# Three edits to a fused attention, feed-forward and soft-expert kernel: when query chains begin, which TensorE work goes first, and where the short key sums stand

## The chip, the cores and the metric

The kernel runs on one core of a Trainium2 chip. The time is the device time of one execution in microseconds (us), the median of three runs. A profile is one more execution, taken by the hardware profiler; its times are its own and are compared with its own total.

## The reference

Three stages follow each other, on 4 x 1088 = 4352 tokens of 128 numbers.

- **Attention by feature maps.** For each of 4 batches and 4 heads, a query or key x of 32 numbers becomes 64 features, phi(x) = outer(S1 x, S2 x), with S1 and S2 of 8 x 32. The keys of a batch are summed up once, kv = sum over the sequence of phi(k) v and z = sum of phi(k); a query's answer is phi(q) kv / (phi(q) z + 1e-6). The sequence of 1088 is 8 x 128 + 64, so each key sum has eight full pieces of 128 rows and one short piece of 64.
- **Gated feed-forward.** x is scaled by its root mean square, then silu(x Wg) * (x Wv) is formed with 1536 hidden numbers and multiplied by Wo back to 128.
- **Soft experts.** logits = x phi with 32 slots; a softmax over all tokens gives each slot's input, 8 experts of two layers process 4 slots each, and a softmax over slots mixes the results for each token. The maximum over all tokens means that this stage ends after the last token of the second.

## The kernel before

The tokens are cut into nine tiles: T = 0 to 7 hold 512 tokens each (two tiles to a batch), and T = 8 holds the 256 that are left over from all batches. A tile's feed-forward runs in 12 slots, one for each 128 hidden columns (`NF` = 12; six double ones for T = 8). In a slot TensorE makes `g` and `v`, three passes of 512 columns each (`mm3`, L692 to L694: high by high, low by high, high by low parts of float32 as two float32r numbers). ScalarE makes `silu` of g (L733) and the rounded `hh` (L743), VectorE the product `hf` (L734) and the rest `hl` (L748), and two slots later TensorE adds three more passes into the output `o`. In tile 0 the output uses whole float32 products instead (L758). So a slot holds nine full matmuls of 128 x 128 weights and 512 columns.

Beside these slots run generators called chains, which are advanced one step at a time; each step says on which phase the next one goes, `PE` or `POST` (the other engines), and how many slots later.

- `k_chain(b)` prepares a batch's keys: VectorE transposes (L366), TensorE projects (L385, L389), VectorE forms the products `work` and `pkr` (L318), TensorE sums them with v (L424, method `sum`; `work` are the full pieces, `pkr` the short ones), ScalarE spreads the sums (L435), TensorE transposes them (L449) and ScalarE places them in `kvz` (L458).
- `q_chain(T)` prepares a tile: VectorE transposes the queries (L542), TensorE projects (L547), VectorE forms the products (L318) and transposes them, TensorE multiplies by `kvz` (`attend`, L579, or L587 for T = 8), VectorE divides (L595 to L598), ScalarE squares (L621), GpSimd takes the root (L628, L629), VectorE scales (L634), TensorE transposes (L640), and ScalarE and VectorE write `xh` and `xl` (L647, L653), which every `g` and `v` of that tile reads.
- `r_chain(T)` makes the logits of a finished tile (L775, L792).

`start_tile(T)`, called in a tile's first slot, issues the loads of the next batch on even T, spawns its key chain, and spawns the query chain of tile T + 1. Tile 0's own chains are written out in the list `FRONT`.

The small TensorE work of a chain step is called a burst here. The engine executes its instructions in the order of its queue, and that order is set when the kernel is built: a scheduler picks among instructions whose predecessors are done by its own estimate, by priority, which is by default the order in which the code was written. `tc.issue_after(i)` keeps an instruction behind i on the engine; `tc.high_priority()` puts it ahead of others that are ready. The function `burst` (L936) runs a chain's PE step behind the burst before it. Only the `attend` of L579 has the higher priority before the change.

Of the kernel before, what the change touches and what calls it, by code (L numbers as in the profile page):

```python
# [21 lines left out]
NF = DFF // P  # L22
# [15 lines left out]
WORDS = "1 2 3 3 3 3 3 4 4 4 3 3 4 4 5 5 5 4 5 5 4 6 6 6 6 6 7 7 7 6 6 7 7 8 8 8 7 8 8 7"  # L38
CONV = 6
LOCK = 3  # L40

WHOLE = NF

PIECE = 256
PE, POST = "pe", "post"
# [4 lines left out]
def body(ctx, tc, q, k, v, s1, s2, wg, wv, wo, rg, phi, w1, w2, out):  # L50
# [19 lines left out]
    def row(tag, bufs=1, dt=F32):  # L70
        return sb.tile([P, 512], dt, tag=tag, name=tag, bufs=bufs)
# [123 lines left out]
    mark = {}  # L195
# [147 lines left out]
    def bank():  # L343
        if not free:
            return aux()
        free.append(free.pop(0))
        tag = free[-1]
        return ps.tile([P, 512], F32, tag=tag, name=tag, bufs=3 if tag == "aux" else 2)

    class Keys:  # L350
# [25 lines left out]
        def project(self, banks=1):  # L376
            for h in range(H):
                if h == 0 or h == 2 and banks == 2:
                    a = bank()
                self.a["k", h // 2] = a  # L380
                cs = slice(P * h, P * h + P)
                for c in range(2) if banks == 2 else (1, 0):
                    with tc.issue_after(self.last) if self.last else nullcontext():
                        o = a[64 * c : 64 * c + 64, cs]
                        self.last = pe.matmul(o, bdk.rearrange("p h r -> p (h r)"), self.kT[c][:, cs], start=True, stop=True).ins  # L385

        def project_r(self):
# [24 lines left out]

        def sum(self, hp, ts, banks=1):

            for t in ts:
                if t == 0 and (hp == 0 or banks == 2):
                    self.a["kv", hp] = self.a["kv"] = bank()
                if banks == 1:
                    self.a["kv", hp] = self.a["kv"]

                for h2 in range(2):
                    h = 2 * hp + h2
                    v0 = D1 * (8 * h + 4 * (t % 2) + t // 2) if t < 8 else D1 * h
                    pe.matmul(  # L424
                        self.a["kv", hp][64 * h2 : 64 * h2 + self.cols, 64 * hp : 64 * hp + 64],
                        (va_all if t < 8 else vr_all)[:, v0 : v0 + self.cols],
                        self.pk[hp][:, h2, t, :] if t < 8 else self.pk[2][:64, h, 0, :],
                        start=(t == 0),
                        stop=(t == 8),
                    )  # L430

        def spread(self):
# [45 lines left out]
    def k_chain(b):  # L478
        k = Keys(b)
        with tc.issue_after(mark["word"]), tc.issue_after(mark["pow"]):  # L480
            k.zero()
            if b == 1:
                pool.memset(kvT[32:64], 0.0)
            for hp in range(2):
                k.copy_v(hp, pool.tensor_copy)
        for c in (0, 1):
            yield POST, 1
            with tc.issue_after(mark["gate"]):
                k.transpose(c)
                if c == 0:  # L490
                    k.transpose(2)
        yield PE, 0
        k.project_r()
        k.project()
        kv_done.discard("free")
        yield POST, 1
        k.turn(slice(0, 2), row("x2"))
        k.halves_r()
        mark["k"] = k.outer(2)
        kv_done.add("free")  # L500
        k.outer(0)
        yield POST, 1
        k.outer(1)
        yield PE, 0
        for hp in range(2):
            k.sum(hp, range(9))
        yield PE, 1
        yield POST, 0
        k.spread()
        yield PE, 0  # L510
        k.back()
        yield POST, 1
        k.place()
        kv_done.add(b)
# [391 lines left out]
    def spawn(c, phase, at=0):  # L906
        chains.append([c, phase, now + at])
# [25 lines left out]
    def burst(*step):  # L933
        traced = nc.cur_bb.bb.instructions
        start = len(traced)
        with tc.issue_after(mark["burst"]) if "burst" in mark else nullcontext():  # L936
            step[0](*step[1:])
        for i in traced[start:]:
            if i.engine == mybir.EngineType.PE:
                mark["burst"] = i  # L940
# [62 lines left out]
    def after_front():  # L1003
        s = ExitStack()
        if now < base + LOCK:
            for i in front_end.values():
# [6 lines left out]
    def start_tile(T):  # L1013
        if T == 6:
            for u in range(2):
                for hf in range(2):
                    load(
                        out=qr[64 * hf : 64 * hf + 64, :, u, :], in_=q[2 * u + hf, :, 1024:, :].rearrange("h p d -> p h d")
                    )
        if T == 2:  # L1020
            with tc.issue_after(mark["word"]), tc.issue_after(mark["pow"]):
                make_own()
                pool.tensor_copy(phi4[:, 1:4], phi4[:, 0:1].to_broadcast([P, 3, NS]))
        if T % 2 == 0 and T // 2 + 1 < B:
            b = T // 2 + 1
            load_k(b)
            load_q(b)
            load_kr(b)
            load_v(b)
            spawn(k_chain(b), PE, 8 if b == 1 else 0)  # L1030
        if T < 8:
            spawn(q_chain(T + 1), POST, 2 if T == 0 else 0)
        else:
            w = work()[:, 0 : 2 * DM].rearrange("p (c n) -> p c n", n=DM)
            h, l = (t[:, NF - 2 :, :].bitcast(F32) for t in (woh, wol))
            pool.tensor_tensor(out=w, in0=h, in1=l, op=ALU.add)
            wo_end.extend((w[:, 0], w[:, 1]))
        if 6 <= T <= 7:
            for e in range(4 * (T - 6), 4 * (T - 6) + 4):
                if e < 5:  # L1040
                    t = ring()
                    load(out=t, in_=w1[e])
                    w1_sb[e] = [t[:, 0:512], t[:, 512:]]
                else:
                    w1_sb[e] = [row(("cvs", "cvc", "cvt")[e - 5], 2) for _ in range(2)]
                    for c in range(2):
                        load(out=w1_sb[e][c], in_=w1[e, :, 512 * c : 512 * c + 512])
            for j in range(2 * (T - 6), 2 * (T - 6) + 2):
                for c in range(2):
                    t = ring() if j < 3 else big("qt", 2)  # L1050
                    w2_sb[j, c] = t.rearrange("p (e c n) -> p e c n", e=2, c=4)
                    for e in range(2):
                        src = w2[4 * e + j, 512 * c : 512 * c + 512]
                        load(out=w2_sb[j, c][:, e], in_=src.rearrange("(c p) n -> p c n", p=P))
# [4 lines left out]
    for i in range(n_slots + LAG):  # L1059
        now = base + i  # L1060
        if i < n_slots:
            T, f = slots[i]
            if "silu" in mark:
                mark["pace"] = mark["silu"]
            ff_in(T, f)
            if f == 0:
                start_tile(T)
        if i == NF - 1:
            conv.append(split_o())
        if i == 0:  # L1070
            ordered[:] = [mybir.EngineType.DVE]
            for e in list(latest):
                if e not in ordered:
                    latest.pop(e)
        if i == 2:
            ordered.clear()
            latest.clear()
        if 1 <= i <= n_slots:
            in_order(ff_low, *slots[i - 1])
        for _ in range(CONV if i else 0):  # L1080
            with after_front():
                in_order(conv_step, 1)
        if i < n_slots:
            in_order(ff_gate, T, f)
            mark.setdefault("pace", mark["silu"])
        for _ in range(0 if i else CONV):
            with after_front():
                in_order(conv_step, 1)
        for c in list(chains):
            with after_front():  # L1090
                in_order(advance, POST, c)
        if i < n_slots:
            in_order(ff_high, T, f)
        if i >= LAG:
            To, fo = slots[i - LAG]
            in_order(ff_out, To, fo)
            if fo == NF - 1 and To < 8:
                if To < 7:
                    spawn(r_chain(To), POST, 1)
                else:  # L1100
                    with tc.high_priority():
                        for _ in r_chain(To):
                            pass
                        a_max()
        for c in list(chains):
            with after_front():
                burst(in_order, advance, PE, c)
# [25 lines left out]
    b, c = aux(), ps.tile([P, 512], F32, tag="v", name="c", bufs=2)  # L1133
# [122 lines left out]
    for o, part, eng in zip(sod, (soh, sol), (act.copy, dve.tensor_copy)):  # L1256
# [7 lines left out]
        for t in range(2):  # L1264
            ts = slice(64 * t, 64 * t + 64)
# [69 lines left out]
```

## Time and profile before

| | us |
|---|---|
| median of 3 runs | 310.29 (310.04 to 311.12) |
| the profiled execution | 309.8 |
| its span, first to last instruction | 307.8 |
| TensorE busy | 297.0 |
| VectorE busy | 235.0 |
| ScalarE busy | 179.1 |
| GpSimd busy | 65.7 |

The profiled execution is 2.0 us longer than the span that its trace covers. A TensorE matmul's row runs from its start to the modelled end of its results, so that rows overlap; how long one holds the engine is read from its start to the next one's start. A float32 matmul stands in the trace as two passes, so x2 of the order is x4 of the trace; the float32r ones of L692 to L694 and the transposes are one.

### The profile page before, as it was taken

What the parts mean: (1) busy time and instruction counts of PE and PEld (TensorE: products, weight loads), DVE (VectorE), ACT (ScalarE), POOL (GpSimd) and SP (SyncE); (2) the same over time, 40 slices, a digit from 0 to 9 for tenths busy, and PEclk for the clock granted to TensorE, in tenths of its full rate; (3) what the DMA queues carried; (4) which work ended last, traced back from release to release, by engine and by line L of the source; (5) the groups of instructions that cost most, each with busy time, mean ns of one, the idle gap of its engine ahead of it and who ended that gap; (6) DMA issues with size and microseconds to landing.
All of it is one profiled execution on the core that took longest, in us unless ns stands there. A gap on an engine that the chain in (4) does not pass through costs nothing.

```text
span 307.8 us, 6343 instructions
## 1 busy us (share of the span) xinstructions
PE 297.0 (96%) x2372; PEld 231.7 (75%) x2372; DVE 235.0 (76%) x461; ACT 179.1 (58%) x400; POOL 65.7 (21%) x111
## 2 busy tenths in 40 slices
PE   7999989999999999999999989999999999999993
PEld 4777655787887778788878867888787878897482
DVE  3989956877888967978699779787985767665862
ACT  2568774476565376755653667556654665466562
POOL 2569899000602010110020200102000000003210
PEclk9999999999999999999999999999999999999998
DMA  5997000010025100010351001001981692000016
GB/s 143 348 337 214 9 1 0 2 24 13 0 78 151 26 2 0 15 21 0 81 152 19 0 3 23 13 0 27 350 205 19 173 320 53 2 0 3 2 51 240
DMA packets 40766, 24.02 MB, mean 78 GB/s; under 512 B 18080, under 2 KB 36768, under 8 KB 40736
## 3 DMA queue, kind: packets, MB, share of 16 engines
q1 hardware_dynamic: 40560, 23.56, 26.7%
q8 instruction: 18, 0.29, 0.4%
q10 hardware_dynamic: 176, 0.07, 0.1%
q14 instruction: 12, 0.10, 0.1%
HBM read 19.81 MB, written 2.23 MB: 72 GB/s over the span
## 4 chain that ended last, share of the span: by engine, by line
PE 78%; DVE 7%; ACT 5%; POOL 4%; issue 2%; DMA 1%; SPq 1%; DVEq 0%; ACTq 0%; POOLq 0%
PE g L692 7%; PE v L692 7%; PE v L693 7%; PE g L693 7%; PE g L694 7%; PE v L694 7%; PE o L694 6%; PE o L692 6%; PE o L693 6%; PE o L758 2%; PE aux L579 2%; POOL wgl L277 2%; PE aux L424 2%; DVE work L318 2%; PE fo L1286 2%
## 5 line engine op out<-in xcount | busy, mean ns | idle before, releaser
L743 ACT CAST hh<-hf 128x512 fp32r<-128x512 f32 x89 | 54.9, 617 | 46.6 <-DVE hf L734 46.1
L733 ACT ACTIVATE silu<-g 128x512 f32<-128x512 f32 (+1 forms) x103 | 60.1, 592 | 36.2 <-PE g L694 35.6
L734 DVE TENSOR_TENSOR hf<-v,silu 128x512 f32<-128x512 f32 (+1 forms) x91 | 61.2, 676 | 16.6 <-PE v L694 6.4
L748 DVE TENSOR_TENSOR hl<-hf,hh 128x512 fp32r<-128x512 f32 x89 | 60.7, 686 | 14.5 <-ACT hh L743 12.7
L692 PE MATMUL g<-xh,wgh 128*128 128x512 f32 (+1 forms) x107 | 43.7, 408 | 1.8 <-ACT xh L647 0.9
L692 PE MATMUL v<-xh,wgh 128*128 128x512 f32 (+1 forms) x107 | 42.6, 398 | 0.4 <-DVE hh L734 0.4
L693 PE MATMUL g<-xh,wgl 128*128 128x512 f32 (+1 forms) x107 | 41.0, 383 | 0.0
L694 PE MATMUL v<-xl,wgh 128*128 128x512 f32 (+1 forms) x107 | 40.7, 380 | 0.0
L693 PE MATMUL v<-xh,wgl 128*128 128x512 f32 (+1 forms) x107 | 40.5, 379 | 0.0
L694 PE MATMUL g<-xl,wgh 128*128 128x512 f32 (+1 forms) x107 | 40.5, 379 | 0.0
L694 PE MATMUL o<-hl,woh 128*128 128x512 f32 (+1 forms) x94 | 36.8, 392 | 0.0
L692 PE MATMUL o<-hh,woh 128*128 128x512 f32 (+1 forms) x94 | 36.6, 389 | 0.0
L693 PE MATMUL o<-hh,wol 128*128 128x512 f32 (+1 forms) x94 | 35.7, 380 | 0.0
L628 POOL TENSOR_SCALAR rs<-ss 128x4 f32<-128x4 f32 (+1 forms) x8 | 2.8, 354 | 123.3 <-ACT sq L621 123.2
L692 PEld LDWEIGHTS g<-xh,wgh 128*128 128x128 f32 x107 | 20.1, 188 | 8.5 <-ACT silu L733 2.8
L692 PEld LDWEIGHTS v<-xh,wgh 128*128 128x128 f32 x107 | 20.1, 188 | 5.8 <-DVE hh L734 1.2
L693 PEld LDWEIGHTS g<-xh,wgl 128*128 128x128 f32 x107 | 20.1, 188 | 4.7 <-POOL wgl L277 0.6
L694 PEld LDWEIGHTS g<-xl,wgh 128*128 128x128 f32 x107 | 20.1, 188 | 4.1 <-issue 0.2
L694 PEld LDWEIGHTS v<-xl,wgh 128*128 128x128 f32 x107 | 20.1, 188 | 4.0
L693 PEld LDWEIGHTS v<-xh,wgl 128*128 128x128 f32 x107 | 20.2, 188 | 3.4 <-issue 0.2
L694 PEld LDWEIGHTS o<-hl,woh 128*128 128x128 f32 x94 | 17.8, 189 | 3.9 <-DVE hl L748 0.4
L692 PEld LDWEIGHTS o<-hh,woh 128*128 128x128 f32 x94 | 17.7, 189 | 3.3 <-issue 0.2
(278 smaller groups left out, 492.8 us busy)
## 6 DMA issues: line engine op xcount, KB each, us to landing
ring<-in_moe_w_dram SPq DMA_DIRECT2D x12, 256.0 KB, 6.6
ring<-in_moe_w_dram SPq DMA_DIRECT2D x5, 512.0 KB, 4.6
ring<-in_k_dram SPq DMA_DIRECT2D x16, 128.0 KB, 3.0
ring<-in_v_dram SPq DMA_DIRECT2D x4, 512.0 KB, 5.4
ring<-in_moe_w_gate_dram SPq DMA_DIRECT2D x6, 256.0 KB, 5.1
ring<-in_moe_w_val_dram SPq DMA_DIRECT2D x6, 256.0 KB, 7.6
ring<-in_moe_w_out_dram SPq DMA_DIRECT2D x3, 512.0 KB, 7.9
qt<-in_q_dram SPq DMA_DIRECT2D x3, 512.0 KB
```

Source lines behind the costliest of these rows:

```text
L277: i = pool.tensor_tensor(out=dl[:, ts], in0=src[:, ts], in1=dh[:, ts].bitcast(F32), op=ALU.subtract)
L318: return on.tensor_tensor(out=dst.rearrange("p g (r s) -> p g r s", s=R), in0=x1.unsqueeze(3).to_broadcast([pp, n, r, R]), in1=x2.unsqueez ...
L424: pe.matmul(self.a["kv", hp][64 * h2 : 64 * h2 + self.cols, 64 * hp : 64 * hp + 64], (va_all if t < 8 else vr_all)[:, v0 : v0 + self.cols] ...
L579: last = pe.matmul(o, pD[rs, f, h, cs], rhs, start=(f == 0), stop=(f == 1)).ins
L692: first = pe.matmul(o, ah, bh, start=start, stop=False)
L693: pe.matmul(o, al, bh, start=False, stop=False)
L694: last = pe.matmul(o, ah, bl, start=False, stop=stop)
L733: mark["silu"] = act.activation(s[:, cs], g[:, cs], AF.Silu).ins
L734: mark["gate"] = mark["gate", T, f] = dve.tensor_tensor(out=hf32[T, f][:, cs], in0=v[:, cs], in1=s[:, cs], op=ALU.mult).ins
L743: act.copy(hh[T, f], hf32[T, f])
L748: dve.tensor_tensor(out=hl[T, f], in0=hf32.pop((T, f)), in1=hh[T, f].bitcast(F32), op=ALU.subtract)
L758: last = pe.matmul(ops[T][:, 0:w], w_c, h[:, cs], start=(c == 0), stop=(c == NF - 1))
```

## The change

Query chains: `start_tile` spawns the chain of tile T + 1 only for T = 0 and 1 (tiles 1 and 2); for T = 1 to 6, the chain of tile T + 2 is spawned in slot 9 of 12 of tile T (`EARLY` = 3), as a step on phase POST. Precedence: everything that `burst` runs, and the key projection (L385), is given the higher priority. Key sums: the second pair's sum now begins with its short piece (8, 0, 1, ... 7), so that it stands next to the short piece with which the first pair ends; the `start` and `stop` marks go by place in the list. The short piece of the keys is transposed behind the second full piece and not the first.

```diff
--- before.py
+++ after.py
@@ -38,6 +38,7 @@
 WORDS = "1 2 3 3 3 3 3 4 4 4 3 3 4 4 5 5 5 4 5 5 4 6 6 6 6 6 7 7 7 6 6 7 7 8 8 8 7 8 8 7"
 CONV = 6
 LOCK = 3
+EARLY = 3
 
 WHOLE = NF
 
@@ -380,8 +381,10 @@
                 self.a["k", h // 2] = a
                 cs = slice(P * h, P * h + P)
                 for c in range(2) if banks == 2 else (1, 0):
-                    with tc.issue_after(self.last) if self.last else nullcontext():
+                    with ExitStack() as s:
+                        s.enter_context(tc.issue_after(self.last) if self.last else nullcontext())
                         o = a[64 * c : 64 * c + 64, cs]
+                        s.enter_context(tc.high_priority())
                         self.last = pe.matmul(o, bdk.rearrange("p h r -> p (h r)"), self.kT[c][:, cs], start=True, stop=True).ins
 
         def project_r(self):
@@ -412,8 +415,8 @@
 
         def sum(self, hp, ts, banks=1):
 
-            for t in ts:
-                if t == 0 and (hp == 0 or banks == 2):
+            for i, t in enumerate(ts):
+                if i == 0 and (hp == 0 or banks == 2):
                     self.a["kv", hp] = self.a["kv"] = bank()
                 if banks == 1:
                     self.a["kv", hp] = self.a["kv"]
@@ -425,8 +428,8 @@
                         self.a["kv", hp][64 * h2 : 64 * h2 + self.cols, 64 * hp : 64 * hp + 64],
                         (va_all if t < 8 else vr_all)[:, v0 : v0 + self.cols],
                         self.pk[hp][:, h2, t, :] if t < 8 else self.pk[2][:64, h, 0, :],
-                        start=(t == 0),
-                        stop=(t == 8),
+                        start=(i == 0),
+                        stop=(i == 8),
                     )
 
         def spread(self):
@@ -487,7 +490,7 @@
             yield POST, 1
             with tc.issue_after(mark["gate"]):
                 k.transpose(c)
-                if c == 0:
+                if c == 1:
                     k.transpose(2)
         yield PE, 0
         k.project_r()
@@ -502,8 +505,8 @@
         yield POST, 1
         k.outer(1)
         yield PE, 0
-        for hp in range(2):
-            k.sum(hp, range(9))
+        k.sum(0, range(9))
+        k.sum(1, (8, *range(8)))
         yield PE, 1
         yield POST, 0
         k.spread()
@@ -933,7 +936,7 @@
     def burst(*step):
         traced = nc.cur_bb.bb.instructions
         start = len(traced)
-        with tc.issue_after(mark["burst"]) if "burst" in mark else nullcontext():
+        with tc.high_priority(), tc.issue_after(mark["burst"]) if "burst" in mark else nullcontext():
             step[0](*step[1:])
         for i in traced[start:]:
             if i.engine == mybir.EngineType.PE:
@@ -1028,9 +1031,9 @@
             load_kr(b)
             load_v(b)
             spawn(k_chain(b), PE, 8 if b == 1 else 0)
-        if T < 8:
+        if T < 2:
             spawn(q_chain(T + 1), POST, 2 if T == 0 else 0)
-        else:
+        if T == 8:
             w = work()[:, 0 : 2 * DM].rearrange("p (c n) -> p c n", n=DM)
             h, l = (t[:, NF - 2 :, :].bitcast(F32) for t in (woh, wol))
             pool.tensor_tensor(out=w, in0=h, in1=l, op=ALU.add)
@@ -1065,6 +1068,8 @@
             ff_in(T, f)
             if f == 0:
                 start_tile(T)
+            if f == NF - EARLY and 0 < T < 7:
+                spawn(q_chain(T + 2), POST)
         if i == NF - 1:
             conv.append(split_o())
         if i == 0:
```

The order on the engines is the same up to the key projection of batch 1, and on TensorE again behind the transpositions of tile 8's queries (L640). In the changed kernel the line numbers stand 1 to 5 later. Three places follow, each before and then changed.

ScalarE, from the last squares of the query chain of tile 5 (sq,ss) to its `xh`; kvT and kvz belong to the key chain of batch 3.

```order
L621 ACTIVATE sq,ss<-x 128x128
L743 CAST hh<-hf 128x512
L733 ACTIVATE silu<-g 128x512
L435 COPY kvT<-aux 33x512 x2
L743 CAST hh<-hf 128x512
L733 ACTIVATE silu<-g 128x512
L743 CAST hh<-hf 128x512
L458 COPY kvz<-aux 32x8x33 x4
L647 ACTIVATE xh<-aux,g_sb 128x512
L313 COPY asb<-aux 128x128
```

The same place, changed: `xh` of tile 5 and then the key chain of batch 3.

```order
L650 ACTIVATE xh<-aux,g_sb 128x512
L746 CAST hh<-hf 128x512
L736 ACTIVATE silu<-g 128x512
L746 CAST hh<-hf 128x512
L438 COPY kvT<-aux 33x512 x2
L746 CAST hh<-hf 128x512
L736 ACTIVATE silu<-g 128x512 x2
L746 CAST hh<-hf 128x512
L461 COPY kvz<-aux 32x8x33 x4
L314 COPY asb<-aux 128x128
```

`xh` stood behind the four copies into `kvz` and stands ahead of both steps of that key chain now.

TensorE, the `attend` of tile 8 (kvr by work).

```order
L694 MATMUL v<-xl,wgh 128x512
L587 MATMUL aux<-kvr,work 64x132 x6
L692 MATMUL o<-hh,woh 128x512
L693 MATMUL o<-hh,wol 128x512
L587 MATMUL aux<-kvr,work 64x132
L692 MATMUL v<-xh,wgh 128x512
L693 MATMUL v<-xh,wgl 128x512
```

The same, changed.

```order
L697 MATMUL v<-xl,wgh 128x512
L590 MATMUL aux<-kvr,work 64x132 x8
L695 MATMUL o<-hh,woh 128x512
L696 MATMUL o<-hh,wol 128x512
L695 MATMUL v<-xh,wgh 128x512
```

Eight matmuls stood in three pieces of six, one and one (the last one ten rows further down) and stand in one now; the `attend` of tiles 2 and 3, in two pieces each before, is whole as well, and so are six projections of queries (L547).

TensorE, the key sums of batch 1 (va by work: full pieces; vr by pkr: short pieces), with the projection of queries behind them.

```order
L758 MATMUL o<-hh,ring 128x512
L424 MATMUL aux<-work,va 33x64 x16
L424 MATMUL aux<-pkr,vr 33x64 x2
L424 MATMUL aux<-work,va 33x64 x16
L424 MATMUL aux<-pkr,vr 33x64 x2
L547 MATMUL aux<-bd,T 128x64 x4
L692 MATMUL g<-xh,wgh 128x512
```

The same, changed.

```order
L697 MATMUL g<-xl,wgh 128x512
L427 MATMUL aux<-work,va 33x64 x16
L427 MATMUL aux<-pkr,vr 33x64 x4
L427 MATMUL aux<-work,va 33x64 x16
L550 MATMUL aux<-bd,T 128x64 x4
L695 MATMUL v<-xh,wgh 128x512
```

The four short matmuls stand side by side between the two sets of full ones, in all three batches that go this way (1 to 3).

## Rows read from the trace of the kernel before

**Rows 1.** The page's first part: busy us, share of the span, instructions.

```profile
PE 297.0 (96%) x2372; PEld 231.7 (75%) x2372; DVE 235.0 (76%) x461; ACT 179.1 (58%) x400; POOL 65.7 (21%) x111
```

**Rows 2.** Chain that ended last, 160 to 186: start us, us, what.

```profile
172.62 1.53 POOL rs L629
...
180.91 0.70 ACT xh L647
```

**Rows 3.** TensorE timeline, 179.4 to 185.6: start us, us, work [idle before <-releaser].

```profile
180.26 0.45 PE L694 MATMUL o<-hl,woh 128*128 128x512 f32 x1
181.65 0.50 PE L692 MATMUL g<-xh,wgh 128*128 128x512 f32 x1 [0.94 <-ACT xh L647]
181.99 0.40 PE L693 MATMUL g<-xh,wgl 128*128 128x512 f32 x1
...
184.30 0.39 PE L694 MATMUL v<-xl,wgh 128*128 128x512 f32 x1
184.75 0.50 PE L692 MATMUL g<-xh,wgh 128*128 128x512 f32 x1
```

**Rows 4.** TensorE timeline, 138.9 to 140: a lone piece of a query projection.

```profile
138.95 0.39 PE L694 MATMUL g<-xl,wgh 128*128 128x512 f32 x1
139.18 0.55 PE L547 MATMUL aux<-bd,T 128*128 128x64 f32 x4
...
139.86 0.39 PE L693 MATMUL g<-xh,wgl 128*128 128x512 f32 x1
```

**Rows 5.** Busy us by engine (instructions), granted clock, DMA share, GB/s, 160 to 170.

```profile
160.00:170.00 10.00, 10.00 (x117) 7.91 (x112) 9.91 (x22) 3.67 (x9) 0.52 (x1) 1.00 0.12 20
```

**Rows 6.** TensorE timeline, 229.9 to 236.6: the attend of tile 8, first two pieces.

```profile
229.93 0.39 PE L694 MATMUL v<-xl,wgh 128*128 128x512 f32 x1
230.25 1.11 PE L587 MATMUL aux<-kvr,work 128*64 128x132 f32 x12
...
231.63 0.40 PE L693 MATMUL o<-hh,wol 128*128 128x512 f32 x1
231.96 0.44 PE L587 MATMUL aux<-kvr,work 128*64 128x132 f32 x2
...
232.66 0.40 PE L693 MATMUL v<-xh,wgl 128*128 128x512 f32 x1
```

**Rows 7.** TensorE timeline, 70.2 to 73: the attend of tile 2, in two pieces.

```profile
70.21 0.39 PE L694 MATMUL o<-hl,woh 128*128 128x512 f32 x1
70.52 0.33 PE L579 MATMUL aux<-kvz,work 64*64 64x66 f32 x4
...
71.12 0.40 PE L693 MATMUL o<-hh,wol 128*128 128x512 f32 x1
71.45 1.15 PE L579 MATMUL aux<-kvz,work 64*64 64x66 f32 x60
...
72.93 0.39 PE L692 MATMUL g<-xh,wgh 128*128 128x512 f32 x1
```

**Rows 8.** TensorE timeline, 164.9 to 166.9: an attend in one piece, L792 behind it.

```profile
164.94 0.39 PE L694 MATMUL g<-xl,wgh 128*128 128x512 f32 x1
165.26 1.16 PE L579 MATMUL aux<-kvz,work 64*64 64x66 f32 x64
...
166.76 0.39 PE L693 MATMUL o<-hh,wol 128*128 128x512 f32 x1
```

**Rows 9.** TensorE timeline, 108.3 to 111.8: the key sums of batch 2.

```profile
108.64 1.09 PE L424 MATMUL aux<-work,va 128*33 128x64 f32 x32
109.66 0.30 PE L424 MATMUL aux<-pkr,vr 64*33 64x64 f32 x4
109.90 1.09 PE L424 MATMUL aux<-work,va 128*33 128x64 f32 x32
```

## The prediction

> **What bounds the kernel now.** First the page's busy times: TensorE is busy 96% of the span, the next engine 76% [rows 1]. Busy alone is weak evidence for an engine whose rows overlap, so the second view is the chain that ended last. Between the front (to about 45 us, which this change leaves as it is) and the tail it is TensorE nearly all the time, with one exception: from 164 to 181.6 us it runs through VectorE, ScalarE and GpSimd, with a root of 1.53 us among its steps, and ends in the 0.70 us that write `xh` [rows 2]. What waits for it is seen in the third view, TensorE's timeline: the first `g` matmul of tile 5 starts at 181.65, with 0.94 us of idle time ahead of it put down to `xh` [rows 3]. So the kernel is bound by how fast TensorE gets through its queue, and once by a query chain that is late. The order in the section on the change says why it is late: `xh` of tile 5 stands on ScalarE behind the whole key chain of batch 3, since both chains are spawned in the same slot, the first of tile 4.
>
> The fourth view is the same timeline read from start to start. Two full matmuls start 0.23 us apart (138.95 to 139.18) [rows 4], whatever their rows' lengths. Any larger distance around small work is a cost of that work. Everything below is such distances; the granted clock was 1.00 in the stretch read for it [rows 5].
>
> **Query chains begun earlier.** Nothing is removed or added: the same instructions are traced in another order. The chain of tile T + 2 begins three slots ahead of tile T + 1, where it began in that tile's first slot. A slot is nine full matmuls, 9 x 0.23 = 2.1 us, so it begins at least 6.2 us earlier, and bursts make it more. What the wait costs: the last matmul before it starts at 180.26, tile 5's first at 181.65, 1.39 us where 0.23 would do: 1.16. The next one comes 0.34 later, 0.11 over. A second wait follows at the head of the same tile (184.30 to 184.75, 0.45 where 0.23 would do: 0.22), since the first `g` waited for the late `xl` pass and `silu` for that [rows 3]. Together 1.49 us. The 6.2 us cover the 1.39 more than four times, so I take the whole 1.49 as gone. The lower bound is nothing (the lateness is handed to another wait, a rival below); there is no more than 1.49 to be had here. For tiles 3, 4, 6, 7 and 8 the edit costs and saves nothing, as the trace has no wait for their `xh`; the cover is that `xh` is written before the tile begins, and starting earlier only widens it.
>
> The moved step's instructions, all of them: a transpose, two products and a transpose, the divisions and the scaling on VectorE, a copy, four squares and `xh` on ScalarE, two small operations on GpSimd, three bursts on TensorE. It issues no DMA. Its queries were loaded in the first slot of tile 2, 4 or 6, nine slots ahead, so SP's queue is moved past nothing it needs; GpSimd's root passes nothing but copies of v and the clearing of `kvz`. What is late next: the key chain of batch 3, which now has VectorE behind the query chain in places. Its own deadline is the `attend` of tile 6, a tile later than that of tile 5 had been, so it has the room that the query chain lacked. VectorE is the doubtful cover: it was busy 9.91 of 10 us from 160 to 170 [rows 5]. The change takes the query chain's VectorE work out of just that stretch and puts it into others.
>
> **Bursts ahead of the rest.** The order shows what the precedence does: pieces become whole. A piece that is split off costs a visit of its own, and its price can be read where a piece stands alone. By the distance from the full matmul before it to the second full matmul after it, less two ordinary distances (0.46):
> - `attend` of tile 8: the piece of twelve passes takes 231.63 - 229.93 - 0.46 = 1.24, a piece of two 232.66 - 231.63 - 0.46 = 0.57 [rows 6]. Ten passes more are 0.67, 0.067 each, so two passes are worth 0.13 and the visit 0.44. There are two such pieces of two: 0.88 saved.
> - `attend` of tile 2: pieces of 4 and 60 passes, the second with L792 behind it, take 0.45 and 1.35 [rows 7]; whole, with L792 behind it, it took 1.36 at 164.94 [rows 8]. Saved 0.44, and the same for tile 3, which is split in the same way: 0.88.
> - Projection of queries (L547), split in two in six tiles: a lone piece of four passes takes 139.86 - 138.95 - 0.46 = 0.45 [rows 4], 0.11 a pass, 0.09 of the whole being the slower start of the full matmul behind it. So six joins save between nothing and 6 x 0.09 = 0.54. I take nothing, since no row of a whole one between full matmuls shows less than 0.11 a pass.
>
> On this last point a rule weighs in: the Trainium skill, TensorEngine Tiling (Array Packing), section Key Properties, says that changing the tiling mode drains TensorE while a change of tile within a mode doesn't. By it the visits of 64-row or 64-column work cost something and the 128 x 128 projections of queries nothing, so these joins would give 0 and not 0.54; the rows agree on the first half (0.44 a visit), and 0.09 is all they leave of the second.
>
> One more visit goes where the key projection of batch 1 stood in two parts around a float32 output matmul: between 0 and 0.44, I take 0.2. Nothing else is added: the number of matmuls stays. The cost of precedence is a wait: a burst that comes to the head of the queue before its input is ready holds up the `g`, `v` and `o` matmuls behind it, and ScalarE and VectorE after them. The trace of before has one place with this precedence already, the `attend` of L579, and no wait of TensorE's on it behind the front, so I take 0; upwards it is bounded by the third rival.
>
> **Key sums side by side.** The block of four short passes takes 109.90 - 109.66 = 0.24, where 32 full ones take 1.02, 0.13 for four [rows 9]. The change of shape is worth 0.11 a block. Of two blocks one is left, in three batches: 3 x 0.11 = 0.33, between 0 (the joined block pays it at its other end) and 0.6 (in and out both saved). I take 0.33. That the short transpose stands behind the second full one moves 0.1 to 0.2 us of VectorE work ahead of a projection that waits for both anyway: 0.
>
> **The sum.** 1.49 + 0.88 + 0.88 + 0 + 0.2 + 0.33 = 3.8 us. The profiled execution took 309.8 (span 307.8 and 2.0 around it, unchanged), so 306.0 by it. The median of the three runs is 0.5 above the profiled one: 310.3 - 3.8 = 306.5.
>
> **Rivals.**
> 1. The wait is handed on. The joined bursts save their 2.3, but a late chain still stops TensorE once for about what it did (1.49), at the key chain or at VectorE's products for the `o` matmuls. For: VectorE full from 160 to 170 [rows 5]. Against: the deadlines of the moved chains lie a slot count of 6 us or more behind. Then 308.0.
> 2. VectorE takes over. TensorE would wait for `hf` and `hl` in the new places where key and query products meet. If one stretch like 160 to 170 at full VectorE stretches by a third, 3.3 us, the sum is nearly spent: 309.8. For: the query chains now fall beside the logits of a finished tile. Against: VectorE is idle 24% of the span [rows 1] and the total is unchanged.
> 3. Precedence makes it slower. Each tile has three bursts that now go first; each waits for a step of VectorE or ScalarE of the kind of `xh`, 0.70 us [rows 2]. If one burst of each of eight tiles comes to the head a whole such step early, TensorE loses 8 x 0.7 = 5.6 us, and the result is 310.3 - 3.8 + 5.6 = 312.1. It decides from 4.8 us on, 0.6 a tile. For: an engine that works in order has no way around. Against: in the order as built each burst still has full matmuls ahead of it since its producer, and in before a burst with precedence shows no wait.
> That the precedence changes nothing is excluded by the order.
>
> **How the numbers follow.** The forecast 0.75, first rival 0.12, second 0.06, third 0.07. The likeliest is 306.5, its own range 305.4 to 307.4: downwards the upper ends of the joins (0.54, 0.24 and 0.27 more), upwards half the wait's price. The range for 8 in 10 goes from 305.3 to 308.7, taking in the first rival and leaving out the other two and a little below. A measurement of this kernel tells a change from none at about 0.3%, 0.9 us, so faster means under 309.4: forecast and first rival, with a small share of the second, 0.88; the same 0.06; slower 0.06.
>
> **What would show it.** Right: no idle time put down to `xh` at the head of tile 5, or any tile behind tile 1; each `attend` one group of 64 passes (16 for tile 8) with one slow start behind it; one block of eight short passes of about 0.35 us in the key sums; all else as far apart as before. The gain should be in two parts, 1.5 at one place and 2.3 in about eight. Wrong: an idle time of TensorE before a burst (L547, L579, L424, L640) put down to VectorE or ScalarE, or `o` matmuls that wait for `hl`. A result over 308.7 would mean that one of these waits is there more than once.

## The result, and the profile after

The changed kernel took 305.74 us, the median of six runs (305.13 to 308.0), against 310.43 for six runs of the kernel before (309.75 to 311.12): a ratio of 0.9867, with an interval of 0.9825 to 0.9909. It is faster, by 4.7 us; 3.8 were forecast.

The profiled execution of the changed kernel is not one of the ordinary ones: it took 308.0 us, as one other of the six did (307.95), while the other four took 305.13 to 306.02. The reason lies in the front, ahead of everything that the change touches. Here is the granted clock there, in the windows from 5 to 10 and 10 to 15 us, first of the changed kernel and then of the one before. The columns are the stretch, its length, the busy time of TensorE, of its weight loads, VectorE, ScalarE and GpSimd, each with its instructions, the granted clock, the share of the DMA engines and GB/s.

```profile
5.00:10.00 5.00, 3.66 (x33) 2.76 (x32) 3.69 (x9) 0.33 (x1) 0.57 (x1) 0.79 0.88 258
10.00:15.00 5.00, 5.00 (x62) 4.00 (x63) 4.89 (x6) 2.42 (x7) 3.77 (x3) 0.52 1.01 316
```

```profile
5.00:10.00 5.00, 3.98 (x42) 2.89 (x41) 4.23 (x10) 0.33 (x1) 1.19 (x1) 1.00 0.92 266
10.00:15.00 5.00, 4.52 (x88) 3.79 (x88) 4.87 (x7) 3.79 (x12) 2.75 (x3) 1.00 1.06 356
```

The column to compare is the third from the end: 0.79 and 0.52 against 1.00, so that TensorE ran for most of the second window at the lower of its two levels (1.2 GHz), and did 62 instructions there where it did 88. Tile 0's first `g` matmul of 512 columns then starts at 26.40 us and not at 23.95, 2.45 us later, with the same instructions in the same order up to there. Executions of the kernel before and of two experiments show a like loss (last section), so it is not the change's. All comparisons of traces start behind it.

From that `g` to the end of TensorE's last matmul the kernel before takes 303.19 - 23.95 = 279.24 us and the changed one 301.18 - 26.40 = 274.78. The change is worth 4.46 us in these two traces; 309.8 - 4.46 is 305.3, where the four ordinary runs are. The page's busy line answers to [rows 1]; the second line gives the granted clock in 40 slices (the dip is the second digit):

```profile
PE 295.9 (97%) x2372; PEld 233.6 (76%) x2372; DVE 234.6 (77%) x461; ACT 179.5 (59%) x400; POOL 63.6 (21%) x111
...
PEclk9599999999999999999999999999999999999999
```

The counts of instructions are those of before, TensorE's 2372 among them. What changed is how they stand. TensorE's timeline of the changed kernel, at the four places that the prediction spoke of (start, us, work):

```profile
73.49 0.39 PE L697 MATMUL o<-hl,woh 128*128 128x512 f32 x1
73.81 1.16 PE L582 MATMUL aux<-kvz,work 64*64 64x66 f32 x64
74.90 0.33 PE L795 MATMUL aux<-ident,lT 128*128 128x128 f32 x1
74.99 0.48 PE L695 MATMUL v<-xh,wgh 128*128 128x512 f32 x1
75.31 0.39 PE L696 MATMUL v<-xh,wgl 128*128 128x512 f32 x1
...
108.56 1.09 PE L427 MATMUL aux<-work,va 128*33 128x64 f32 x32
109.58 0.41 PE L427 MATMUL aux<-pkr,vr 64*33 64x64 f32 x8
109.92 1.09 PE L427 MATMUL aux<-work,va 128*33 128x64 f32 x32
...
179.10 0.39 PE L697 MATMUL v<-xl,wgh 128*128 128x512 f32 x1
179.32 0.39 PE L695 MATMUL g<-xh,wgh 128*128 128x512 f32 x1
179.55 0.39 PE L696 MATMUL g<-xh,wgl 128*128 128x512 f32 x1
...
229.01 0.39 PE L697 MATMUL v<-xl,wgh 128*128 128x512 f32 x1
229.33 1.17 PE L590 MATMUL aux<-kvr,work 128*64 128x132 f32 x16
230.43 0.50 PE L695 MATMUL o<-hh,woh 128*128 128x512 f32 x1
230.77 0.40 PE L696 MATMUL o<-hh,wol 128*128 128x512 f32 x1
```

In their order: the `attend` of tile 2 is one group of 64 passes, where [rows 7] shows 4 and 60. The short key sums are one block of eight, 0.34 us from start to start, where [rows 9] shows one of two blocks of four. Tile 5's first `g` (179.32) starts 0.22 after the matmul ahead of it, with no idle time, where it was 1.39 [rows 3]. The `attend` of tile 8 is one group of 16 passes, where [rows 6] shows pieces. The `xh` of tile 5, in ScalarE's timeline, ends at 166.75 + 0.69 = 167.44, so it lies ready 11.9 us before that `g`:

```profile
166.75 0.69 ACT L650 ACTIVATE xh<-aux,g_sb 128x512 fp32r<-128x512 f32 x1
```

TensorE's list of waits for the whole span (work, releaser: us in total, times, longest) has no `xh` any more:

```profile
...
PE aux L388 <- DVE T L367: 1.2, 1, 1.2
PE g L695 <- ACT silu L736: 0.8, 2, 0.4
PE fo L1291 <- ACT wgh L844: 0.7, 1, 0.7
PE v L695 <- DVE hh L737: 0.4, 1, 0.4
PE aux L643 <- DVE x L637: 0.3, 1, 0.3
...
```

These five, and the two left out, lie ahead of 46 us or behind 283 us. Between these, some 237 us pass in which the list has no wait of TensorE's on a chain, a burst or `hl`.

### The profile page after: what moved, and what is told of

Read it like the earlier page. It is cut to its first block, busy times and chain, and to the rows that moved or that the text cites. A ratio compares the mean times of both kernels' runs of the same rounds, so it can differ in the third digit from the quotient of the medians.

```text
span 306.2 us, 6349 instructions
## 1 busy us (share of the span) xinstructions
PE 295.9 (97%) x2372; PEld 233.6 (76%) x2372; DVE 234.6 (77%) x461; ACT 179.5 (59%) x400; POOL 63.6 (21%) x111
## 4 chain that ended last, share of the span: by engine, by line
PE 84%; DVE 4%; POOL 4%; ACT 3%; DMA 1%; issue 1%; SPq 1%; DVEq 0%; ACTq 0%
PE o L697 7%; PE v L695 7%; PE g L695 7%; PE o L695 7%; PE v L697 7%; PE v L696 7%; PE g L696 7%; PE g L697 7%; PE o L696 7%; PE aux L427 2%; PE aux L582 2%; PE o L761 2%; PE aux L550 2%; POOL wgl L278 2%; PE fo L1291 2%; POOL hf L233 1%
## 5 line engine op out<-in xcount | busy, mean ns | idle before, releaser
L736 ACT ACTIVATE silu<-g 128x512 f32<-128x512 f32 (+1 forms) x103 | 60.8, 593 | 45.1 <-PE g L697 44.5
L695 PE MATMUL v<-xh,wgh 128*128 128x512 f32 (+1 forms) x107 | 41.9, 391 | 0.4 <-DVE hh L737 0.4
L631 POOL TENSOR_SCALAR rs<-ss 128x4 f32<-128x4 f32 (+1 forms) x8 | 1.9, 240 | 134.3 <-ACT sq L624 134.2
```

What stands on the lines that cost most here:

```text
L695: first = pe.matmul(o, ah, bh, start=start, stop=False)
L736: mark["silu"] = act.activation(s[:, cs], g[:, cs], AF.Silu).ins
```

## The experiments

The prediction left two questions. It gave the vanished wait to the earlier query chains and the joined `attend`s to the precedence, but both came from reading one order in which all three edits were made at once. And the price of a small visit was read from distances in one trace. The first three kernels do one part of the change alone, the fourth leaves one out, the fifth varies a size, the sixth is on the front, and the last two put a known number of visits in. The whole change without the precedence, or without the key sums, was not run. Where a saving is given behind the front, it is the 279.24 us of the kernel before less the same stretch in the trace of the kernel named.

**Early query chains alone.** The kernel before, with the spawn of the change and nothing else:

```diff
-        if T < 8:
+        if T < 2:
             spawn(q_chain(T + 1), POST, 2 if T == 0 else 0)
-        else:
+        if T == 8:
...
+            if f == NF - EARLY and 0 < T < 7:
+                spawn(q_chain(T + 2), POST)
```

> The kernel before with the early query chains alone. Theory A (the parts add up: early chains take away the wait of 1.6 us at the head of tile 5, precedence and the sums' order take away visits): the wait is gone, and of the visits only the second piece of tile 3's attend (0.46), as the order shows tile 2's still in two pieces and tile 8's in three: 310.4 - 2.1 = 308.3. Rival B (precedence is what speeds the late chain up; the early start only moves it): the wait stays or comes back at another tile, 309.5 to 310.4.

Measured: 308.59 us (12 runs, 307.38 to 311.37) against 310.3 (29 runs), ratio 0.9943 [0.9909, 0.9976]. Behind the front its trace saves 1.83 us. The theory's wait is gone: from 45 to 280 us no row of TensorE has an idle time ahead of it, and in its list of waits the feed-forward's `g` waits only for `silu`, in tile 0:

```profile
PE g L693 <- ACT silu L734: 0.8, 2, 0.4
```

The `attend` of tile 3 stands in one piece here, without any precedence; the order had shown that before the run, but the prediction had given it to the precedence.

**Precedence alone.** The kernel before, with the higher priority in the two places:

```diff
+                        s.enter_context(tc.high_priority())
...
-        with tc.issue_after(mark["burst"]) if "burst" in mark else nullcontext():
+        with tc.high_priority(), tc.issue_after(mark["burst"]) if "burst" in mark else nullcontext():
```

> The kernel before with the precedence of bursts alone. By the order tile 8's attend is whole (1.08), tile 3's too (0.46), tile 2's is still in two pieces and tile 5's is newly split (-0.45): 1.1 us of visits. Theory A: the wait for xh of tile 5 stays, because xh still stands behind the copies of the key chain of batch 3 on ScalarE: 309.3. Rival B: the wait goes as well, since each burst of that chain gets through sooner: 307.7.

Measured: 307.55 us (12 runs, 306.58 to 310.87), ratio 0.9907 [0.9878, 0.9936]. Behind the front its trace saves 2.67 us. That is the rival: the wait is gone here too but for a small rest, though each query chain begins where it did. TensorE's timeline at the head of tile 5 (this profile is 3.9 us later as a whole, by its front; see the last section), and then ScalarE's:

```profile
183.23 0.39 PE L695 MATMUL o<-hh,wol 128*128 128x512 f32 x1
183.46 0.39 PE L696 MATMUL o<-hl,woh 128*128 128x512 f32 x1
183.72 0.50 PE L694 MATMUL g<-xh,wgh 128*128 128x512 f32 x1
```

```profile
182.57 0.38 ACT L460 COPY kvz<-aux 32x264 f32<-32x264 f32 x1
182.97 0.69 ACT L649 ACTIVATE xh<-aux,g_sb 128x512 fp32r<-128x512 f32 x1
```

`xh` still stands behind the last copy into `kvz`, and ends at 182.97 + 0.69 = 183.66; the first `g` starts at 183.72, only 0.03 us later than an unhindered one would. With the slower starts that follow at the head of this tile, 0.36 us is left of the wait: from 183.46 to 187.73 there are seventeen distances, 4.27 us where 3.91 would do. So the chain stands where it did in the order, but it gets through sooner: from tile 4's first `g` to the end of this `xh` the kernel before takes 35.37 us (146.23 to 181.60) and this one 34.05 (149.61 to 183.66). Which of its steps gained that stays open.

The `attend` of tile 8 is in one piece in this kernel. So is that of tile 3, while that of tile 5 is newly split:

```profile
106.75 1.16 PE L581 MATMUL aux<-kvz,work 64*64 64x66 f32 x64
...
167.06 0.33 PE L581 MATMUL aux<-kvz,work 64*64 64x66 f32 x4
...
167.99 1.15 PE L581 MATMUL aux<-kvz,work 64*64 64x66 f32 x60
```

That of tile 2 still stands in pieces of 4 and 60 (74.36 and 75.29 in this trace), so precedence did not join it.

**Key sums alone.** The kernel before, with the order of the sums and the later short transpose:

```diff
-                if c == 0:
+                if c == 1:
                     k.transpose(2)
...
-        for hp in range(2):
-            k.sum(hp, range(9))
+        k.sum(0, range(9))
+        k.sum(1, (8, *range(8)))
```

> The kernel before with the order of the key sums and the later short transpose alone. Three blocks of short passes less (3 x 0.12 = 0.36); by the order the key projection of batch 1 stands together (0.35) and tile 2's attend is whole (0.45), tile 3's is not: 1.2 us, 309.2, and the wait at tile 5 stays, by theory A and by rival B alike. If only the switches within the sums count and the other joins are worth nothing: 310.0.

Measured: 309.27 us (12 runs, 308.5 to 313.89), ratio 0.9958 [0.9936, 0.998], as forecast. Its profiled execution took 310.1, and behind the front its trace saves only 0.15 us, so the 1.0 by the medians doesn't show there. The wait is there, in the list of TensorE's waits:

```profile
PE g L692 <- ACT xh L647: 0.9, 1, 0.9
```

The rows at the head of tile 5 tell where the savings went in this trace:

```profile
178.72 0.48 PE L694 MATMUL o<-hl,woh 128*128 128x512 f32 x1
179.53 0.50 PE L692 MATMUL o<-hh,woh 128*128 128x512 f32 x1 [0.33 <-ACT hh L743]
...
181.68 0.50 PE L692 MATMUL g<-xh,wgh 128*128 128x512 f32 x1 [0.92 <-ACT xh L647]
```

At 178.72, counted from tile 0's first `g` (24.40), TensorE is 1.22 us ahead of the kernel before (179.49, from 23.95); at 181.68 it is 0.42 ahead. It came sooner to inputs that were not ready sooner, and waited longer: what is saved ahead of a wait that another engine sets can be lost in it. Whether the runs near the median do the same, no trace shows.

This edit also joined what the prediction gave to the precedence: the key projection of batch 1 stands together in this kernel, and so does the `attend` of tile 2 (64 passes at 71.83). Which of its two halves did that, the sums or the transpose, was not tried apart.

**The whole change without the early chains.**

```diff
-        if T < 2:
+        if T < 8:
...
-            if f == NF - EARLY and 0 < T < 7:
+            if f == NF - EARLY and 0 < T < 0:
```

> The changed kernel without the early query chains (precedence and sums stay). Visits by the order: tile 8's attend 1.08, tile 2's 0.45, key projection 0.35, sums 0.36, tile 5's attend newly split -0.45: 1.8 us. Theory A: the wait of 1.6 us at tile 5 stays: 308.6. Rival B: it is gone with precedence alone: 307.0. In both the changed kernel, at 305.3 to 305.7, is faster.

Measured: 306.75 us (6 runs, 306.31 to 306.94), ratio 0.9869 [0.9837, 0.99]. Again the rival: 306.75 and not 308.6. TensorE at the head of tile 5 and at the `attend` of tile 3, then ScalarE at that head:

```profile
101.00 0.33 PE L582 MATMUL aux<-kvz,work 64*64 64x66 f32 x4
...
102.62 1.15 PE L582 MATMUL aux<-kvz,work 64*64 64x66 f32 x60
...
179.10 0.39 PE L697 MATMUL o<-hl,woh 128*128 128x512 f32 x1
179.33 0.48 PE L695 MATMUL g<-xh,wgh 128*128 128x512 f32 x1
```

```profile
178.57 0.69 ACT L650 ACTIVATE xh<-aux,g_sb 128x512 fp32r<-128x512 f32 x1
```

`xh` ends at 179.26 and its `g` starts at 179.33, 0.23 after the matmul ahead: no idle time, but nothing to spare either: 0.07 us lie between the two, and 0.05 did where `g` waited for `xh` (181.60 to 181.65 in the kernel before). By the slower starts that follow, 0.31 us is left of the wait here (179.10 to 183.32, seventeen distances). What the early chains add in the whole change is that rest and two `attend`s: without them those of tiles 3 and 5 are in two pieces (4 and 60), twice about 0.45. Together that is 1.2 us. Behind the front the two traces differ by 275.90 - 274.78 = 1.12, and the medians by 306.75 - 305.74 = 1.0; the ratios (0.9869 and 0.9867), each against its own runs of before, do not tell the two apart, so this is shown by the rows and traces.

**One slot early and not three.**

```diff
-EARLY = 3
+EARLY = 1
```

> The changed kernel with the query chains begun one slot ahead of the next tile and not three. The wait removed was 1.4 us late and a slot is 2.1 us, so by theory A one slot is enough: 305.7, as the changed kernel within 0.4, no idle time at the head of a tile. If the three slots are needed to get out of the key chain's way on VectorE (rival), the wait is back in part: 306.4 to 307.2.

Measured: 305.44 us (5 runs, 305.16 to 306.32) against 309.95 (9 runs), ratio 0.9852 [0.9835, 0.9869]. The `xh` of tile 5 ends at 170.70 + 0.69 = 171.39 and is first read at 178.45, so some 7 us are to spare; one slot does what three do.

**Small matmuls in the front.** Ten steps of matmuls that compute nothing ahead of the first key projection:

```diff
-n:17 b n:3 kz kt:0 bm kt:1 bm qs kp kt:2 kx:0 ...
+n:17 b n:3 kz kt:0 bm kt:1 bm qs n:10 kp kt:2 kx:0 ...
```

> The changed kernel with ten more filler matmuls on TensorE ahead of the first key projection, where the profile of the changed kernel has 1.2 us of idle time and then the half clock until about 14.5 us. Ten fillers are 1.1 us at 0.11 each. If it is that idle time that brings the half clock: no run has a granted clock under 0.99, and the times are 305.3 in all runs. If the half clock comes of something else: some runs at 0.987 and 308 as before. If the fillers delay the key projection by more than they cover: 305.5 to 306.4 in all.

Measured: 305.64 us (4 runs, 305.4 to 305.88), ratio 0.9858 [0.9842, 0.9875], with mean clocks of 0.996 to 0.998. No run shows the loss in the front. But none of the five runs of the kernel with one slot shows it either (305.16 to 306.32), and that one has no such filling, so this tells nothing of the cause, and the filling gained nothing else.

**36 lone visits of 64 x 64.** The changed kernel, with a float32 matmul of 64 columns ahead of the `g` of every second slot of tiles 2 to 7, into the bank of that `g`, which overwrites it:

```diff
+                if m == 0 and 2 <= T < 8 and f % 2:
+                    o = store[T, f][0]
+                    pe.matmul(o[0:64, 0:64], ident[0:64, 0:64], ident[0:64, 0:64], start=True, stop=True)
```

> The changed kernel with 36 more small matmuls of 64 x 64 weights and 64 columns, each alone between full matmuls (their results are overwritten). By the price of a visit in another array shape, 0.44 and two passes of work: 36 x 0.47 = 17 us more, 322.5. If a lone burst costs only its passes: 36 x 0.1 = 4 us, 309.3.

Measured: 322.87 us (one run), 17.1 above the changed kernel and 17.4 above the kernel with one slot, which ran on the same chip. One of the visits in TensorE's timeline:

```profile
97.77 0.39 PE L697 MATMUL v<-xl,wgh 128*128 128x512 f32 x1
98.09 0.33 PE L730 MATMUL g<-ident 64*64 64x64 f32 x2
98.34 0.50 PE L695 MATMUL g<-xh,wgh 128*128 128x512 f32 x1
98.68 0.39 PE L696 MATMUL g<-xh,wgl 128*128 128x512 f32 x1
```

From 97.77 to 98.68 are 0.91 us, less 0.46 for two ordinary distances: 0.45 a visit, and the others that stand alone between full matmuls take 0.44 to 0.46. 36 of them are 16.2; some 1 us of the difference is not in the visits.

**The same 36 visits with the whole array.**

```diff
-                    pe.matmul(o[0:64, 0:64], ident[0:64, 0:64], ident[0:64, 0:64], start=True, stop=True)
+                    pe.matmul(o[:, 0:64], ident, ident[:, 0:64], start=True, stop=True)
```

> The same 36 places with small matmuls of 128 x 128 weights and 64 columns, the shape of the array that the full ones have. If only the change of shape costs: 0.11 a pass, two passes, 36 x 0.22 = 8 us more, 313.5. If any lone burst costs a visit: 36 x 0.5 = 18 us or more, over 322.

Measured: 315.14 us (one run).

```profile
97.07 0.40 PE L697 MATMUL v<-xl,wgh 128*128 128x512 f32 x1
97.30 0.33 PE L730 MATMUL g<-ident 128*128 128x64 f32 x2
97.44 0.48 PE L695 MATMUL g<-xh,wgh 128*128 128x512 f32 x1
97.76 0.40 PE L696 MATMUL g<-xh,wgl 128*128 128x512 f32 x1
```

0.69 - 0.46 = 0.23 a visit, 0.11 a pass, as in [rows 4]; 36 are 8.3, and the run is 9.4 to 9.7 longer than the same two, so 1.1 to 1.4 us of it are not in the visits. The two kernels have the same number of passes, of the same type and the same 64 columns, at the same places. What differs is the part of the array used, and the smaller part costs 0.22 us a visit more although the matmul is a quarter of the size. Whether it is the fewer rows or the fewer columns was not tried apart. The rows show it on both sides: at 64 x 64 the small matmul starts 0.32 us after the full one ahead of it (0.23 with the whole array), and the full one behind starts 0.25 after the small one (0.14).

## Why the prediction was right, and where it was not

**The sum held, and in the right places.** By distances from full matmul to full matmul in the two traces, as the prediction took them, its terms came out so:

| term | forecast | measured |
|---|---|---|
| wait at the head of tile 5 | 1.49 | 1.60 |
| `attend` of tile 8 joined | 0.88 | 1.08 |
| `attend`s of tiles 2 and 3 joined | 0.88 | 0.91 |
| L547 joined | 0 | 0 |
| key projection of batch 1 | 0.2 | 0.35 |
| short key sums side by side | 0.33 | 0.36 |
| sum | 3.8 | 4.3 |

The two traces differ by 4.46, so 0.16 us are left for small differences of spacing. The 1.60 is the prediction's 1.49 and one more slow start, behind the matmul at 184.75 (0.34 to the next, 0.11 over). Two other terms were too small. For tile 8 the prediction credited the joined passes with 0.067 each at the new place, but the whole `attend` of 16 passes took 1.30 (the rows at 229.01 and 230.77: 1.76 - 0.46), where 12 had taken 1.24 alone [rows 6]: the added four cost 0.06 in all. For the key projection it took 0.2, the middle of what it knew of a visit (0 to 0.44), and the stretch gave 0.35 (3.40 us before, 3.05 after).

**The price of a visit was about right, and it hangs on the part of the array used.** The prediction read 0.44 without the passes, from pieces of 128 x 64 [rows 6]. The 64 x 64 visits put in took 0.45 with their two passes, as the lone piece in [rows 7] did with four; at 0.018 a pass (60 of that shape take 1.08 us, from 71.45 to 72.53) that is 0.41 without them. That the joins of L547 would save nothing, and not 0.54, holds where it was read: for tile 3 the whole one took 1.34 us with the transposes beside it (83.49 to 85.29, less 0.46), and the two pieces 1.12 and 0.22 (80.68 to 82.26 and 83.88 to 84.56). The Trainium skill, TensorEngine Tiling (Array Packing), section Key Properties, says that a change of tiling mode drains the engine and a change of tile alone does not. The two kernels with 36 visits agree with it in the cost: 0.45 with the smaller part of the array, and 0.23 with the whole one, which is the price of two passes [rows 4]; that a drain is what takes the time, no row shows.

**What failed is the attribution to single edits.** The prediction gave the whole wait to the chain that begins 6.2 us earlier, and read in the order "what the precedence does: pieces become whole". The runs show otherwise:

- The wait goes with the early chains alone, and with the precedence alone too. It has two remedies in one change, and they are not equal. With precedence and no early chains `xh` is done just when TensorE comes to it, and 0.31 to 0.36 us of the 1.60 stays; with the early chains nothing stays, and `xh` lies ready 11.9 us in the whole change.
- `attend` of tile 2 and the key projection of batch 1 were joined by the edit to the key sums, which the prediction priced by its short blocks alone (0.33); alone it is worth 1.0 by the medians. `attend` of tile 3 is whole with the early chains alone and with the precedence alone, and split where precedence and key sums go together without the early chains. That of tile 8 is whole in every kernel with the precedence and split in the two without it.
- So the parts are not independent. Alone, early chains and precedence each take the wait and each join the `attend` of tile 3 (0.46), and the precedence splits that of tile 5 (0.45), which stays whole with the early chains. By the medians the three save 1.7, 2.75 and 1.0, 5.5 in all, and together 4.7; behind the front their traces save 1.83, 2.67 and 0.15, 4.65 in all, and together 4.46. The intervals reach 0.7 to 1.3 us either way, so it is the rows that show the overlap, not these sums.

The sum did not suffer, since it was made from the order of the whole change, and that order was the one that ran. Had the question been what each edit is worth alone, the prediction's 1.49, 1.96 (its two pairs of `attend`s and the key projection) and 0.33 would have stood against 1.7, 2.75 and 1.0.

**The rivals.** The handed-on wait (308.0), VectorE as the bound (309.8) and the precedence that holds up the queue (312.1) all asked for a new idle time of TensorE behind the front, and there is none: from 46 to 283 us no row has one, and the two waits behind that, 0.2 and 0.7 us, are those of before. VectorE's total is 234.6 us against 235.0.

## What to carry to other kernels

Where an engine is never idle, price small work by the distance between the large instructions around it, and look in the order as built for pieces that could stand together: here each lone piece with another shape of the array cost 0.45 to 0.57 us, and joined to its burst four such passes cost 0.06. Where a scheduler sets the order, take each edit's worth from runs with it alone and with it left out: for the early chains the two are 1.83 and 1.12 us by the traces, and they are made of different rows. A wait whose input comes just in time is gone by the chance of the order, so read how long its input lay ready before calling it settled. And what is saved ahead of a wait that another engine sets can be lost in it.

## What the runs showed of the hardware

The loss in the front was not expected. In the profiled run of the changed kernel TensorE stood idle for 1.21 us ahead of the first key projections, which start at 7.38, and the granted clock was 0.52 from 10 to 15 us, at the cost of 2.45 us; the run of before had stood idle for 1.02 us at that place and kept 1.00. Runs with a mean clock of 0.986 to 0.988 occur with the kernel before (one at 311.9) and with the early chains alone (3 of 12, 310.4 to 311.4) as well.

The profiled run of the precedence alone (310.87 us) lost still more, 3.9 us up to tile 0's first `g` (27.82 against 23.95), and the clock column doesn't show it: it has 1.00 in every window there, and the run's mean is 0.997. The pace of the matmuls does. This trace, and then the kernel before:

```profile
5.95 0.69 PE L387 MATMUL aux<-T,bdk 128*64 128x128 f32 x2
7.55 0.90 PE L387 MATMUL aux<-T,bdk 128*64 128x128 f32 x5 [0.91 <-DVE T L366]
...
12.71 1.98 PE L426 MATMUL g<-work,va 128*64 128x64 f32 x32
```

```profile
5.70 0.43 PE L385 MATMUL aux<-T,bdk 128*64 128x128 f32 x2
7.15 0.54 PE L385 MATMUL aux<-T,bdk 128*64 128x128 f32 x5 [1.02 <-DVE T L366]
...
10.34 1.15 PE L424 MATMUL g<-work,va 128*64 128x64 f32 x32 [0.27 <-ACT va L374]
```

The 32 passes take 1.98 us, as they do at 12.06 in the changed kernel's trace with its clock of 0.50 (12 to 14 us), and not 1.15. So a mean clock near 1 does not rule this loss out. And the slow pace is there at 5.95 already, ahead of the idle time before the key projection, so in this run that idle time did not bring it.

What decides it stays open: the filled front had no such run in four, but the front without filling had none in five either.
